# Two matmul stages on one core: a part of the weight preparation is moved behind the sums of an item

## The chip, the cores and the metric

The kernel runs on one core of a Trainium2 chip. The core has five engines that run side by side, each with its own queue of instructions in program order: PE (TensorE, the matmul engine, with a separate record PEld for its weight loads), DVE (VectorE), ACT (ScalarE), POOL (GpSimd) and SP (SyncE, which starts the transfers here). An engine waits where an operand that another engine makes is not there yet, and everything behind the waiting instruction on that engine waits too. The metric is the device time of one execution in microseconds. Three timed runs of the kernel before took 768.05, 769.60 and 771.38 us: 769.6 is the median.

## The reference

Attention with a learned bias over positions, and behind it a two-layer network with a squared relu, all in float32. `_attn_ref` makes `attn_out` of 4 batches x 8 heads x 576 positions x 64; it is laid out as `x` of 2304 tokens x 512, and then:

```python
def _moe_ref(x, w_in, w_out):
    h = x @ w_in              # 512 -> 2048
    r = np.maximum(h, 0.0)
    g = r * r
    return (g @ w_out)        # 2048 -> 512
```

In the attention part `scores = scale * q k^T + bias`, where the bias is a small network of the distance of two positions, then softmax and a product with `v`. The change leaves that part alone.

## The kernel before

The first half of the program (to some 376 us) is the attention part; beside it eight of the sixteen `w_in` tiles are prepared. The second half is a loop over 40 items, written by hand in the order in which each engine is to run it (`with tc.manual_schedule()`, L954 on): no scheduler reorders it.

An item is a pair (n, P): n is a block of tokens (four of 512, worked as 256 columns by a seven-product scheme, and a fifth, half as wide, of what is left), P is one of eight pieces of the hidden dimension. `runs` says in which order they come: items 0 to 3 are block 0 with P 0 to 3, items 4 to 7 block 1, 8 to 11 block 2, 12 to 17 block 3, and so on; the last eight items are the narrow block. For an item i the loop issues

- `products(i)`: on PE, 24 matmuls into the PSUM tile `ha` and 18 into `hb` (L851). Both tiles exist once, so they can be written only when the sums of item i-1 have read them.
- `parts_g(i - 1)`: the squared result of the item before is split in a high part `gh` (a cast on ACT, L887) and the rest `gl` (a subtraction on DVE, L888), two halves each.
- `lead(m)` for the weight tiles m that `lead_at` gives this item: one ACT operation (L176) and four DVE operations on the bits of a raw weight tile (L179 to L182) that put together the tile `wa`.
- `sums(i)`: ACT writes `s` from `ha` (L865), and four DVE operations (L867 to L870) combine `ha`, `hb` and `s` to `c`. The first two read `ha`, the others `hb`.
- `high_out(m)` for a `w_out` tile: a cast on ACT (L778) and a subtraction on POOL (L779). For a `w_in` tile: `sums_in` on POOL (L789 to L791), `high_in` on ACT (L800), `low_in` on DVE (L804), and the fetch of the next raw tile.
- `high_x`, `low_x`, `sums_x` in the items of `split_at`: the split of a coming block of tokens (L825 on ACT, L832 on DVE, L819 on POOL).
- `squares(i)`: relu and square on ACT (L876, L877) for items below `GA`, one DVE operation (L879) for the others.
- `down(i - 1)`: on PE, 24 matmuls into `y` for a full-width item (L943), with `gh`, `gl` and the two `w_out` tiles of the piece. Behind the last item of a run, `leave` copies `y` out.

A block's scale is found in two steps. `x_largest` (four DVE reductions, L185) stands in items 4, 8 and 28; `set_scale` stands in the item after. The latter calls `power` (L187): one more small reduction on DVE (L185), a one-column matmul that spreads the result over the partitions (L194, into a free column of `hb`), and four tiny DVE operations that read it (L195 to L199) and one more (L600). The matmul L194 stands on PE between `products(i)` and `down(i - 1)`.

In the kernel before, `set_scale` is issued ahead of `parts_g`, and all the `lead` calls of an item ahead of its `sums`. Items 1, 2 and 3 have two `w_out` tiles each; items 4, 5, 8, 9, 12 to 15 and 18 to 25 have one tile each.

Of the kernel before, what the change touches and what calls it, by code (L numbers as in the profile page):

```python
# [36 lines left out]
MD, K0, E2, BW, KP, PN, KA = 0x15555, 2, 1, 1, 2, 1, 1  # L37
C0, ND, NG, GA, QA, WU, QS = 2, 2, 4, 18, 12, 32, 2
BO, B1 = (3, 5, 8, 10, 13, 15, 18, 20), (12, 3, 8)
# [12 lines left out]
AH = 2  # L52
ND = 3
NG = 4
GA = 26
KA = 4
QA = 0
WU = 12
# [19 lines left out]
def attention_then_relu2_mlp(ctx: ExitStack, tc: tile.TileContext, q, k, v, cols, w_in, w_out, psi, xmat, dist, out):  # L78
# [92 lines left out]
    def lead_w(n, a):  # L171

        raw = wraw_t.pop(n)
        low, high = (raw[:, :, :, t] for t in range(2))
        af = a.bitcast(F32)
        ins = ACT.activation(out=af, in_=high.bitcast(F32), func=AF.Abs)  # L176
        if n in early:
            tc.keep_in_program_order(ins)
        DVE.tensor_scalar(out=af, in0=af, scalar1=HI_MIN, scalar2=HI_MAX, op0=ALU.max, op1=ALU.min)  # L179
        DVE.tensor_scalar(out=a, in0=a, scalar1=3, scalar2=0x3FFFFFFF, op0=ALU.logical_shift_left, op1=ALU.bitwise_and)  # L180
        DVE.scalar_tensor_tensor(out=a, in0=high, scalar=-0x40000000, in1=a, op0=ALU.bitwise_and, op1=ALU.bitwise_or)  # L181
        DVE.scalar_tensor_tensor(out=a.bitcast(U32), in0=low.bitcast(U32), scalar=29, in1=a.bitcast(U32), op0=ALU.logical_shift_right, op1=ALU.bitwise_or)  # L182
# [55 lines left out]
    def is_in(n):  # L238
        return n // 2 % 2 == 0
# [344 lines left out]
    def take(x, o, n):  # L584
        o += 18 * S * x
        return area[:, o:o + n]
# [65 lines left out]
    for s in range(NU + TL + 1):  # L652
# [43 lines left out]
        if s < AB * HP * TAIL:  # L696
            n, r = divmod(s, AB * HP)
# [33 lines left out]
    NI = len(items)  # L731
# [3 lines left out]
    stays = (4, 7)  # L735

    lead_at = {1: (6, 7), 2: (10, 11), 3: (14, 15)}
    lead_at.update(zip((4, 5, 8, 9, 12, 13, 14, 15), ((n,) for n in range(16, 24))))
    lead_at.update(zip(range(18, 26), ((n,) for n in range(24, 32))))
    split_at = {0: (1, (2, 5, 3, 4)), 3: (1, (1, 6, 7))}  # L740
    split_at.update({i + j: (n, ms) for i, n in ((6, 2), (10, 3), (30, B)) for j, ms in enumerate(((2, 5, 3, 4), (1, 6, 7)))})
# [14 lines left out]
    def fetch_out(n):  # L756
        fetch(n, home[n].tile([128, 1024], F32, name=f"r{n}", tag=f"w{n}", bufs=1))
# [11 lines left out]
    def lead(n):  # L769
        a = stage_p["p"].tile([128, 2, 256], F32, name="wa", tag="wa", bufs=2)  # L770
        lead_w(n, a.bitcast(I32))
        scratch[n] = a

    def high_out(n):
        a = scratch[n].rearrange("p g n -> p (g n)")
        t = home[n].tile([128, 2, 512], F32R, name=f"w{n}", tag=f"w{n}", bufs=1)
        hi, lo = t[:, 0], t[:, 1]
        ACT.copy(hi, a)  # L778
        POOL.tensor_tensor(out=lo, in0=a, in1=hi.bitcast(F32), op=ALU.subtract)  # L779
        w_t[n] = (hi, lo)  # L780

    def blocks_in(n):
        a = scratch[n].rearrange("p g (a b) -> p (g a) b", b=128)
        return a, zraw[n][:, 0:640].rearrange("p (a b) -> p a b", b=128)

    def sums_in(n):
        a, z = blocks_in(n)
        tt = POOL.tensor_tensor
        tt(out=z[:, 0:2], in0=a[:, 0:2], in1=a[:, 2:4], op=ALU.subtract)  # L789
        tt(out=z[:, 2:4], in0=a[:, 1:3], in1=a[:, 2:4], op=ALU.add)  # L790
        tt(out=z[:, 4], in0=a[:, 0], in1=a[:, 3], op=ALU.add)  # L791
# [47 lines left out]
    def products(i):  # L839
        n, P = items[i]  # L840
        w = width[n]
        ha = ph_p.tile([128, 4, 256], F32, name="ha", tag="ha")
        hb = ph_p.tile([128, 4, 256], F32, name="hb", tag="hb")
        for ms, h in (((2, 3, 4, 5), ha), ((1, 6, 7), hb)):
            for s, m in enumerate(ms):
                k = 0
                for c in range(2):
                    wh, wl = (x[:, LEFT[m]] for x in w_t[4 * P + c])
                    xh, xl = (x[:, c] for x in xs_t[n, m])
                    for a, x in ((wh, xh), (wh, xl), (wl, xh)):  # L850
                        PE.matmul(h[:, s, :w], lhsT=a, rhs=x, start=(k == 0), stop=(k == 5))  # L851
                        k += 1
        return ha, hb

    def sums(i, ha, hb):
        n, P = items[i]
        w = width[n]
        alpha = alpha_t[n]
        if i % 2:
            c, s = (take(1, o, 1024).rearrange("p (m t) -> p m t", m=4)[:, :, :w] for o in (4480, 5504))  # L860
        elif i < NP // 2:
            c, s = (tmp_p.tile([128, 4, 256], F32, name=x, tag=x) for x in "cs")
        else:
            c, s = (xT[1][:, :, 256 * x:256 * x + w] for x in range(2))
        ACT.activation(out=s, in_=ha[:, :, :w], func=AF.Identity, scale=alpha)  # L865
        stt = DVE.scalar_tensor_tensor
        stt(out=c[:, 2:4], in0=ha[:, 1:3, :w], scalar=alpha, in1=s[:, 0:4:3], op0=ALU.mult, op1=ALU.subtract)  # L867
        stt(out=c[:, 0:2], in0=ha[:, 2:4, :w], scalar=alpha, in1=s[:, 0:2], op0=ALU.mult, op1=ALU.add)
        stt(out=c[:, 2:4], in0=hb[:, 0:1, :w].to_broadcast([128, 2, w]), scalar=alpha, in1=c[:, 2:4], op0=ALU.mult, op1=ALU.add)
        stt(out=c[:, 2:4], in0=hb[:, 1:3, :w], scalar=alpha, in1=c[:, 2:4], op0=ALU.mult, op1=ALU.add)  # L870
        c_t[i] = c

    def squares(i):
        c = c_t[i]
        if i < GA:
            ACT.activation(out=c, in_=c, func=AF.Relu)  # L876
            ACT.activation(out=c, in_=c, func=AF.Square)  # L877
        else:
            DVE.scalar_tensor_tensor(out=c, in0=c, scalar=0.0, in1=c, op0=ALU.max, op1=ALU.mult)  # L879

    def parts_g(i):
        c, w = c_t[i], width[items[i][0]]
        for f in range(2):
            gh = mlp.tile([128, 2, 256], F32R, name="gh", tag="gh", bufs=2)[:, :, :w]
            gl = mlp.tile([128, 2, 256], F32R, name="gl", tag="gl", bufs=2)[:, :, :w]
            g = c[:, 1 - f:4:2]
            ACT.copy(gh, g)  # L887
            DVE.tensor_tensor(out=gl, in0=g, in1=gh.bitcast(F32), op=ALU.subtract)  # L888
            g_t[i, f] = (gh, gl)
# [64 lines left out]
    with tc.manual_schedule():  # L954
        for n in first_outs:
            fetch_out(n)
        for n in (6, 7, 10, 11, 14, 15):
            fetch_out(n)
        fetch_in(raw_ins.pop(0))
        sums_x(*split_at[0])  # L960
        for n in first_outs:
            lead(n)
            high_out(n)
        for i in range(NI + 1):
            if i == NP // 2:
                tmp_stack.close()
                late = ctx.enter_context(tc.tile_pool(name="late", bufs=1, side="right", reuse_waits="tile"))
                home.update({n: late for n in (4 * NP - 2, 4 * NP - 1)})
            n, P = items[min(i, NI - 1)]
            if i:  # L970
                fetch_y(i - 1)
            if i < NI:
                ha, hb = products(i)
            if scales and scales[0][0] == i:
                _, m, cols = scales.pop(0)
                set_scale(m, cols, hb[:, 3, 0:1])
            if i:
                parts_g(i - 1)
            for m in lead_at.get(i, ()):
                lead(m)  # L980
            if i < NI:
                sums(i, ha, hb)
            for m in lead_at.get(i, ()):
                if is_in(m):
                    sums_in(m)
                else:
                    high_out(m)
            if i in split_at:
                high_x(*split_at[i])
            if i == 12:  # L990
                keep_tails()
            for m in lead_at.get(i, ()):
                if is_in(m):
                    high_in(m)
                    low_in(m)
                    if raw_ins:
                        fetch_in(raw_ins.pop(0))
            if 4 <= i and raw_outs:
                fetch_out(raw_outs.pop(0))
            if i in split_at:  # L1000
                low_x(*split_at[i])
            if i + 1 in split_at:
                sums_x(*split_at[i + 1])
            if i in largest_at:
                scales.append((i + 1, largest_at[i], x_largest(largest_at[i])))
            if i < NI:
                squares(i)
            if i < NI and (n, P) in firsts:
                r = run_of[n, P]
                if P == 0 and n < B:  # L1010
                    store_x(n)
                if r + 2 < len(runs) and runs[r + 1][1] and r + 1 not in stays:
                    load_x(runs[r + 1][0])
            if i:
                down(i - 1)
# [50 lines left out]
```

## Time and profile before

| | |
|---|---|
| timed runs | 768.05, 769.60, 771.38 us |
| profiled execution, its own time | 769.3 us |
| its span, first to last instruction | 767.5 us |
| mean granted TensorE clock | 0.97 |
| PE busy | 718.7 us, 94% |
| DVE busy | 556.6 us, 73% |
| ACT busy | 463.1 us, 60% |
| POOL busy | 171.8 us, 22% |

The span leaves 1.8 us of the execution outside. The busy share is a mean over the two halves of the program, which have different limits, so what counts for a part of the program is where PE stands idle in it and what ended that. [...] Matmul ends are modelled, so the start of one matmul to the start of the next says more than a single duration.

### The profile page before, as it was taken

Reading aid. Unit: us, or ns where it says so; the run is one execution under the profiler, and the core shown is the slowest. Engines: PE = TensorE matmul, PEld = TensorE weight load, DVE = VectorE, ACT = ScalarE, POOL = GpSimd, SP = SyncE. Lnnn points to the kernel's source line nnn. Section 1 sums busy time; section 2 is a strip of 40 time slices with the busy share of each in tenths; the row PEclk is TensorE's granted clock in tenths of the full one; section 3 lists DMA queues with packets and bytes.
Section 4 is the critical chain, followed back from the end, with each engine's and each line's share of the span. In section 5 each row is a group of like instructions: output and inputs, shape, how many; then the busy total and the mean of one; then the engine's idle time right before and its main releaser. Section 6 shows DMA issues by size and latency. Waiting matters only on the chain.

```text
span 767.5 us, 18176 instructions
## 1 busy us (share of the span) xinstructions
PE 718.7 (94%) x7382; PEld 576.5 (75%) x7382; DVE 556.6 (73%) x1184; ACT 463.1 (60%) x934; POOL 171.8 (22%) x281
## 2 busy tenths in 40 slices
PE   6889999999989999879988999999999999999992
PEld 5767877877756777657776787888888888878881
DVE  6689878775767677897588896777458876669651
ACT  4367787877646678878665685776466554223220
POOL 1464333231210023452014230401001111001000
PEclk7599999999999999999999999999999999999997
DMA  7530000000487522200530446032018332533100
GB/s 212 171 91 18 5 15 2 3 2 18 118 301 225 188 63 88 86 28 2 169 120 1 172 172 233 1 122 86 1 55 312 112 126 97 206 110 111 56 2 27
DMA packets 31607, 75.33 MB, mean 98 GB/s; under 512 B 5540, under 2 KB 13732, under 8 KB 30500
## 3 DMA queue, kind: packets, MB, share of 16 engines
q1 hardware_dynamic: 31524, 74.17, 28.4%
q8 instruction: 58, 0.95, 0.5%
q14 instruction: 25, 0.20, 0.1%
HBM read 55.81 MB, written 18.35 MB: 97 GB/s over the span
## 4 chain that ended last, share of the span: by engine, by line
PE 74%; DVE 12%; ACT 4%; DMA 3%; issue 3%; POOL 2%; SPq 0%; DVEq 0%; ACTq 0%; POOLq 0%
PE y L943 24%; PE ha L851 11%; PE px L505 9%; PE sp L431 8%; PE hb L851 8%; PE pp L487 6%; PE bb L379 4%; DMA stage<-in_w_in 2%; PE bb L398 2%; DVE mask L368 1%; DVE t L437 1%; DVE wa L181 1%; ACT p L442 1%; PE pa L490 1%; ACT pt L488 1%
## 5 line engine op out<-in xcount | busy, mean ns | idle before, releaser
L943 PE MATMUL y<-w,gh 128*128 128x512 f32 x576 | 182.1, 397 | 0.3 <-ACT gh L887 0.2
L851 PEld LDWEIGHTS <-area 128*128 128x128 f16 x1680 | 148.5, 98 | 31.8 <-issue 8.7
L442 ACT ACTIVATE p<-t,negm 128x576 f32<-128x576 f32 x144 | 111.1, 774 | 25.1 <-DVE negm L437 25.0
L437 DVE CUSTOM_DVE_ANT_0 t<-sp,area 128x576 f32<-128x576 f32 x144 | 103.9, 751 | 29.8 <-PE sp L431 25.4
L943 PEld LDWEIGHTS y<-w,gh 128*128 128x128 f32 x576 | 105.2, 188 | 21.4 <-ACT gh L887 0.8
L943 PE MATMUL y<-w,gl 128*128 128x512 f32 x288 | 113.4, 394 | 2.3 <-DVE gl L888 2.3
L431 PE MATMUL sp<-k,q 64*128 64x288 f32 (+1 forms) x640 | 103.2, 432 | 10.2 <-DVE negm L437 6.3
L488 ACT COPY pt<-pp 128x512 f32<-128x512 f32 x144 | 79.5, 582 | 35.3 <-PE pp L487 35.0
L505 PE MATMUL px<-pt,v 128*64 128x128 f32 (+1 forms) x1600 | 97.3, 267 | 2.6 <-DVE bt L385 1.2
L505 PEld LDWEIGHTS px<-pt,v 128*64 128x64 f32 x1600 | 79.5, 137 | 19.5 <-issue 6.4
L851 PE MATMUL ha<-area 128*128 128x256 f16 (+1 forms) x816 | 86.4, 263 | 5.7 <-ACT area L825 2.2
L487 PE MATMUL pp<-ident,p 128*128 128x128 f32 x576 | 84.3, 283 | 2.8 <-ACT pt L488 1.2
L431 PEld LDWEIGHTS sp<-k,q 64*128 64x128 f32 (+1 forms) x640 | 54.5, 177 | 32.1 <-issue 10.6
L487 PEld LDWEIGHTS pp<-ident,p 128*128 128x128 f32 x576 | 62.1, 142 | 20.4 <-issue 10.5
L390 POOL TENSOR_TENSOR area<-bt,bt 128x256 f32<-128x256 f32 x72 | 54.2, 776 | 73.2 <-DVE bt L385 73.2
L368 DVE TENSOR_TENSOR mask<-sdist,theta 128x1024 f16<-128x1024 f16 x81 | 55.8, 725 | 14.8 <-PE bb L398 8.7
L943 PEld LDWEIGHTS y<-w,gl 128*128 128x128 f32 x288 | 54.1, 188 | 16.3 <-DVE gl L888 4.5
L851 PE MATMUL hb<-area 128*128 128x256 f16 (+1 forms) x612 | 64.7, 260 | 0.0
L888 DVE TENSOR_TENSOR gl<-area,gh 128x512 fp32r<-128x512 f32 (+1 forms) x40 | 25.1, 655 | 32.6 <-ACT gh L887 30.9
L779 POOL TENSOR_TENSOR w<-wa,w 128x512 fp32r<-128x512 f32 x16 | 20.9, 1307 | 115.0 <-ACT w L778 115.0
L379 PE MATMUL bb<-wmov,mask 128*128 128x64 f16 x1152 | 40.7, 196 | 0.5 <-DVE bt L385 0.3
L379 PEld LDWEIGHTS <-mask 128*128 128x128 f16 x1152 | 37.0, 100 | 5.4 <-issue 3.9
(171 smaller groups left out, 970.6 us busy)
## 6 DMA issues: line engine op xcount, KB each, us to landing
stage<-in_w_in SPq DMA_DIRECT2D x24, 512.0 KB, 4.3
r<-in_w_out SPq DMA_DIRECT2D x16, 512.0 KB, 5.6
xs<-area SPq DMA_DIRECT2D x4, 1792.0 KB, 9.7
py<-o SPq DMA_DIRECT2D x12, 512.0 KB, 3.5
o<-py SPq DMA_DIRECT2D x12, 512.0 KB, 4.1
v<-in_v SPq DMA_DIRECT2D x16, 320.0 KB, 4.0
q<-in_q SPq DMA_DIRECT2D x32, 128.0 KB, 3.5
zw<-in_w_in SPq DMA_DIRECT2D x8, 512.0 KB, 3.5
```

The source lines that it names most:

```text
L368: DVE.tensor_tensor(out=out, in0=win, in1=th, op=ALU.is_ge)
L379: PE.matmul(bb[:, 64 * (7 - r):64 * (8 - r)], lhsT=m[:, r], rhs=wmov[:, n], start=(n == 0), stop=(n == 1))
L390: POOL.tensor_tensor(out=dst, in0=tw, in1=sw, op=ALU.add)
L431: mm = PE.matmul(out_t[to, x, :HALF], lhsT=qt[rows, cols], rhs=kt[rows, k0:k0 + HALF], start=True, stop=True)
L437: DVE.tensor_tensor_reduce(out=t.rearrange("p (x n) -> p x n", x=2), in0=sp[:, :, :HALF], in1=bias.rearrange("p (x n) -> p x n", x=2), sca ...
L442: ACT.activation(out=p[:, S * n:S * n + S], in_=t, func=AF.Exp, bias=negm[:, n:n + 1], scale=-1.0, accum_out=sums[:, 2 * ic + n:2 * ic + n ...
L487: PE.transpose(pp[:, 128 * c:128 * c + 128], p[:, k0:k0 + 128], ident)
L488: ACT.copy(pt[:, 4 * h:4 * h + 4], pp.rearrange("p (c m) -> p c m", c=4))
L505: PE.matmul(px[64 * h:64 * h + 64, :w], lhsT=vt[:, c, h], rhs=src, start=(c == 0), stop=(c == 4))
L851: PE.matmul(h[:, s, :w], lhsT=a, rhs=x, start=(k == 0), stop=(k == 5))
L888: DVE.tensor_tensor(out=gl, in0=g, in1=gh.bitcast(F32), op=ALU.subtract)
L943: PE.matmul(y_t[n][k], lhsT=a[:, slot, o:o + 128], rhs=x, start=((n, P) in firsts and f == 0 and m == 0), stop=((n, P) in lasts and f == 1 ...
```

## The change

There are four edits. In an item with two weight tiles the first one's bit operations stay ahead of `sums`, and the second's go behind it; the second's cast and subtraction go behind `squares`. `set_scale` is issued behind `sums` instead of ahead of `parts_g`. The table `lead_at` gives no tile to items 4 and 8, and two tiles to items 14 and 15. `GA` is 32 instead of 26, so items 26 to 31 have relu and square on ACT.

```diff
--- before.py
+++ after.py
@@ -52,7 +52,7 @@
 AH = 2
 ND = 3
 NG = 4
-GA = 26
+GA = 32
 KA = 4
 QA = 0
 WU = 12
@@ -735,7 +735,7 @@
     stays = (4, 7)
 
     lead_at = {1: (6, 7), 2: (10, 11), 3: (14, 15)}
-    lead_at.update(zip((4, 5, 8, 9, 12, 13, 14, 15), ((n,) for n in range(16, 24))))
+    lead_at.update({5: (16,), 9: (17,), 12: (20,), 13: (21,), 14: (18, 19), 15: (22, 23)})
     lead_at.update(zip(range(18, 26), ((n,) for n in range(24, 32))))
     split_at = {0: (1, (2, 5, 3, 4)), 3: (1, (1, 6, 7))}
     split_at.update({i + j: (n, ms) for i, n in ((6, 2), (10, 3), (30, B)) for j, ms in enumerate(((2, 5, 3, 4), (1, 6, 7)))})
@@ -971,20 +971,20 @@
                 fetch_y(i - 1)
             if i < NI:
                 ha, hb = products(i)
+            if i:
+                parts_g(i - 1)
+            one, *two = lead_at.get(i, (None,))
+            if one is not None:
+                lead(one)
+            if i < NI:
+                sums(i, ha, hb)
             if scales and scales[0][0] == i:
                 _, m, cols = scales.pop(0)
                 set_scale(m, cols, hb[:, 3, 0:1])
-            if i:
-                parts_g(i - 1)
-            for m in lead_at.get(i, ()):
+            if one is not None:
+                (sums_in if is_in(one) else high_out)(one)
+            for m in two:
                 lead(m)
-            if i < NI:
-                sums(i, ha, hb)
-            for m in lead_at.get(i, ()):
-                if is_in(m):
-                    sums_in(m)
-                else:
-                    high_out(m)
             if i in split_at:
                 high_x(*split_at[i])
             if i == 12:
@@ -1005,6 +1005,8 @@
                 scales.append((i + 1, largest_at[i], x_largest(largest_at[i])))
             if i < NI:
                 squares(i)
+            for m in two:
+                high_out(m)
             if i < NI and (n, P) in firsts:
                 r = run_of[n, P]
                 if P == 0 and n < B:
```

On DVE, in item 2 (`c` and `s` are its sums, `r_6547` and `r_6549` the raw tiles of its two `w_out` tiles), the program stands so before:

```order
L179 TENSOR_SCALAR wa<-wa 128x512
L180 TENSOR_SCALAR wa<-wa 128x512
L181 SCALAR_TENSOR_TENSOR wa<-r_6547,wa 128x512
L182 SCALAR_TENSOR_TENSOR wa<-r_6547,wa 128x512
L179 TENSOR_SCALAR wa<-wa 128x512
L180 TENSOR_SCALAR wa<-wa 128x512
L181 SCALAR_TENSOR_TENSOR wa<-r_6549,wa 128x512
L182 SCALAR_TENSOR_TENSOR wa<-r_6549,wa 128x512
L867 SCALAR_TENSOR_TENSOR c<-ha,small,s 128x512
L868 SCALAR_TENSOR_TENSOR c<-ha,small,s 128x512
L869 SCALAR_TENSOR_TENSOR c<-hb,small,c 128x512
L870 SCALAR_TENSOR_TENSOR c<-hb,small,c 128x512
```

and so now:

```order
L179 TENSOR_SCALAR wa<-wa 128x512
L180 TENSOR_SCALAR wa<-wa 128x512
L181 SCALAR_TENSOR_TENSOR wa<-r_6547,wa 128x512
L182 SCALAR_TENSOR_TENSOR wa<-r_6547,wa 128x512
L867 SCALAR_TENSOR_TENSOR c<-ha,small,s 128x512
L868 SCALAR_TENSOR_TENSOR c<-ha,small,s 128x512
L869 SCALAR_TENSOR_TENSOR c<-hb,small,c 128x512
L870 SCALAR_TENSOR_TENSOR c<-hb,small,c 128x512
L179 TENSOR_SCALAR wa<-wa 128x512
L180 TENSOR_SCALAR wa<-wa 128x512
L181 SCALAR_TENSOR_TENSOR wa<-r_6549,wa 128x512
L182 SCALAR_TENSOR_TENSOR wa<-r_6549,wa 128x512
```

The four sums moved ahead of the second tile's four bit operations; items 1 and 3 read alike.

On DVE around the scale in item 5 (`xT_4285` is the block whose largest value is sought, `xT_77` the result of item 4, `zw` the raw `w_in` tile), before:

```order
L804 SCALAR_TENSOR_TENSOR area<-zw,small,area 128x640
L185 TENSOR_REDUCE small<-xT_4285 128x1 x4
L185 TENSOR_REDUCE small<-small 128x1
L195 TENSOR_SCALAR small<-hb 128x1
L197 TENSOR_SCALAR small<-small 128x1
L198 TENSOR_SCALAR small<-small 128x1
L199 TENSOR_SCALAR small<-small 128x1
L600 TENSOR_TENSOR small<-small 128x1
L888 TENSOR_TENSOR gl<-xT_77,gh 128x512 x2
L179 TENSOR_SCALAR wa<-wa 128x512
L180 TENSOR_SCALAR wa<-wa 128x512
L181 SCALAR_TENSOR_TENSOR wa<-zw,wa 128x512
```

and now:

```order
L185 TENSOR_REDUCE small<-xT_4285 128x1 x4
L888 TENSOR_TENSOR gl<-xT_77,gh 128x512 x2
L179 TENSOR_SCALAR wa<-wa 128x512
L180 TENSOR_SCALAR wa<-wa 128x512
L181 SCALAR_TENSOR_TENSOR wa<-zw,wa 128x512
L182 SCALAR_TENSOR_TENSOR wa<-zw,wa 128x512
L867 SCALAR_TENSOR_TENSOR area<-ha,small,area 128x512
L868 SCALAR_TENSOR_TENSOR area<-ha,small,area 128x512
L869 SCALAR_TENSOR_TENSOR area<-hb,small,area 128x512
L870 SCALAR_TENSOR_TENSOR area<-hb,small,area 128x512
L185 TENSOR_REDUCE small<-small 128x1
L195 TENSOR_SCALAR small<-hb 128x1
```

The small reduction `small<-small` and what follows it moved behind `gl`, the bit operations and the four sums of item 5. In item 9 it is the same; in item 29 there are no bit operations. 

On PE at the same place in item 5 (with what each instruction waits for), before:

```order
L851 MATMUL hb<-area 128x256
L194 MATMUL hb<-small,ones 128x1 [waits DVE_49]
L943 MATMUL y_7163<-w_6565,gh 128x512 [waits Activation_49]
L943 MATMUL y_7163<-w_6565,gh 128x512
L943 MATMUL y_7163<-w_6565,gl 128x512 [waits DVE_49]
```

and now:

```order
L851 MATMUL hb<-area 128x256
L194 MATMUL hb<-small,ones 128x1 [waits DVE_49]
L943 MATMUL y_7148<-w_6565,gh 128x512 [waits Activation_49]
L943 MATMUL y_7148<-w_6565,gh 128x512
L943 MATMUL y_7148<-w_6565,gl 128x512
```

The order on PE did not move: L194 still waits for DVE ahead of the first `y`. What DVE has to do before it is another thing now, and `gl` needs no wait of its own any more.

On ACT the second `abs` (L176) of items 1 to 3 moved behind the first cast, and the second cast (L778) from ahead of relu and square (L876, L877) to behind them, ahead of `gh` (L887).

## Rows read from the trace of the kernel before

**Rows 1.** Windows: from:to, length, busy PE PEld DVE ACT POOL, PEclk, DMA, GB/s
```profile
381.70:419.40 37.70, 32.66 (x199) 26.03 (x200) 30.98 (x47) 21.65 (x31) 10.74 (x9) 0.95 0.21 76
441.10:451.20 10.10, 10.10 (x68) 8.46 (x68) 9.83 (x13) 9.12 (x12) 4.12 (x4) 1.00 0.79 302
429.50:441.10 11.60, 10.85 (x70) 8.68 (x69) 10.60 (x23) 7.96 (x13) 2.23 (x4) 1.00 0.72 275
471.40:483.00 11.60, 10.69 (x70) 8.59 (x70) 6.50 (x15) 4.16 (x7) 1.70 (x2) 1.00 0.63 226
674.70:686.20 11.50, 10.59 (x69) 8.61 (x68) 7.50 (x16) 2.17 (x3) 0.00 (x0) 1.00 0.52 182
```

**Rows 2.** PE timeline: start, length, engine, line, operands, count, [idle before, releaser]
```profile
218.42 1.24 PE L431 MATMUL sp<-k,q 64*128 64x288 f32 x8 [2.48 <-DVE negm L437]
...
340.95 1.24 PE L431 MATMUL sp<-k,q 64*128 64x288 f32 x8 [2.30 <-DVE negm L437]
...
394.31 4.42 PE L851 MATMUL ha<-area 128*128 128x256 f16 x24 [2.10 <-DVE area L868]
...
419.35 2.79 PE L851 MATMUL ha<-area 128*128 128x256 f16 x24 [2.25 <-ACT area L825]
...
471.35 2.79 PE L851 MATMUL ha<-area 128*128 128x256 f16 x24
...
475.95 0.28 PE L194 MATMUL hb<-small,ones 128*128 128x1 f32 x2
...
477.71 0.50 PE L943 MATMUL y<-w,gl 128*128 128x512 f32 x1 [0.91 <-DVE gl L888]
```

**Rows 3.** DVE timeline of item 1
```profile
386.04 1.29 DVE L888 TENSOR_TENSOR gl<-c,gh 128x512 fp32r<-128x512 f32 x2 [0.27 <-issue]
...
390.42 1.79 DVE L181 SCALAR_TENSOR_TENSOR wa<-r,wa 128x512 int32<-128x512 int32 x1
...
392.85 0.74 DVE L867 SCALAR_TENSOR_TENSOR area<-ha,small,area 128x512 f32<-128x512 f32 x1
...
394.94 0.75 DVE L870 SCALAR_TENSOR_TENSOR area<-hb,small,area 128x512 f32<-128x512 f32 x1
```

**Rows 4.** DVE timeline of items 8, 9 and 29
```profile
470.50 0.16 DVE L185 TENSOR_REDUCE small<-small 128x1 f32<-128x4 f32 x1
...
478.18 0.42 DVE L179 TENSOR_SCALAR wa<-wa 128x512 f32<-128x512 f32 x1
...
480.43 0.74 DVE L867 SCALAR_TENSOR_TENSOR area<-ha,small,area 128x512 f32<-128x512 f32 x1
...
684.43 1.23 DVE L879 SCALAR_TENSOR_TENSOR area<-area 128x1024 f32<-128x1024 f32 x1
```

**Rows 5.** POOL timeline of item 1
```profile
390.37 1.29 POOL L779 TENSOR_TENSOR w<-wa,w 128x512 fp32r<-128x512 f32 x1 [17.62 <-ACT w L778]
```

**Rows 6.** ACT timeline behind the sums of item 1
```profile
395.73 1.06 ACT L876 ACTIVATE area<-area 128x1024 f32<-128x1024 f32 x1 [2.10 <-DVE area L870]
...
397.90 1.14 ACT L887 CAST gh<-area 128x512 fp32r<-128x512 f32 x2
```

**Rows 7.** ACT timeline of item 9
```profile
472.08 1.17 ACT L887 CAST gh<-xT 128x512 fp32r<-128x512 f32 x2
473.12 0.70 ACT L176 ACTIVATE wa<-r 128x512 f32<-128x512 f32 x1
474.18 1.11 ACT L865 ACTIVATE area<-ha,small 128x1024 f32<-128x1024 f32 x1 [0.36 <-PE ha L851]
```

**Rows 8.** Windows behind the four PE gaps over 2 us after start-up
```profile
220.20:223.20 3.00, 3.00 (x15) 2.01 (x15) 2.38 (x7) 1.99 (x5) 0.00 (x0) 0.50 1.03 414
341.00:344.00 3.00, 3.00 (x37) 2.31 (x37) 2.79 (x8) 2.68 (x8) 2.51 (x4) 1.00 0.45 160
394.30:397.30 3.00, 2.99 (x15) 2.07 (x16) 1.36 (x2) 1.54 (x2) 0.67 (x1) 0.50 0.00 0
419.40:422.40 3.00, 3.00 (x28) 2.68 (x29) 2.96 (x5) 2.72 (x4) 0.63 (x1) 1.00 0.00 0
```

## The prediction

> **What bounds the kernel now.** I read the page's busy rows first: TensorE (PE) 94% busy over the span, VectorE (DVE) 73%, ScalarE (ACT) 60%. The diff touches only the second half of the program, the loop over 40 items, so I cut that half by item. An item that nothing disturbs takes 10.1 us and PE is busy in all of it; items 1 to 3 together take 37.7 us with PE idle for 5 us; items 5, 9 and 29 take 11.6, 11.6 and 11.5 us [rows 1]. No other full-width item has a gap, so these six are the places where time can be won or lost, and a change elsewhere has to lengthen something past 10.1 us before it is seen.
>
> Then the PE timeline says what those gaps are [rows 2]. Items 2 and 4 begin late because `ha` may not be overwritten before the sums of the item before have read it; the second of these is put down to an ACT operation that ends when the sums do. In items 5, 9 and 29 the scale of a coming block is computed: a one-column matmul (L194) stands behind `hb`, and the down product behind it waits 0.9 us for `gl` (item 9; about as long in 5 and 29).
>
> **The first edit: the second tile's bit operations go behind the sums (items 1 to 3).** On DVE item 1 now runs gl, four bit operations, four more, then sums [rows 3]. The first sum starts at 392.85, and what PE waits for is the second (L868). The second set of bit operations is dear because its L181 takes 1.79 us, against 0.7 for the same line in a set that runs alone (start to start of the set 478.18 to 480.43 is 2.25 us, [rows 4]); GpSimd (POOL) subtracts the first tile's low half from 390.37 to 391.66 [rows 5], and DVE's operation ends only after it. Putting the sums ahead of that set takes about 3.4 us from the way to `ha`, more than the longest gap of 2.25 us, so these gaps go. If nothing else became late the three items would take 3 x 10.1 = 30.3 us, a gain of 7.4.
>
> What is late next is the ring through the second tile: end of sums, relu and square 2.17 us (395.73 to 397.90), a cast for the second tile of about 0.6 (it now stands between square and `gh`), `gh` 0.6 for its first half [rows 6], gl 1.29, one set of bit operations 2.25, sums 2.84 (392.85 to 394.94 and 0.75) [rows 3, 4]: 9.8 us, below 10.1. But POOL subtracts the second tile right when gl wants to start, for 1.29 us [rows 5], while gh lasts 0.6: gl can be held some 0.6 us more, and the ring is 10.4. Adding the one 1.1 us hold that L181 shows gives 11.5. I take 0.6 us of remaining wait in each of three items, 1.8 in all (0 to 4.2). So the first edit gives -5.6 us (-7.4 to -3.2). The 1.6 us of slow clock in item 2 (below) is already in the 37.7.
>
> [...]
>
> **The same edit moves the scale behind the sums (items 5, 9 and 29), and this is the costly part.** Before, the small reduction that L194 reads came directly behind the reductions of the block, an item early: at 470.50, with PE asking at 475.95 [rows 2, 4]. It now stands on DVE behind gl, one set of bit operations and four sums of the item itself. L194 still stands on PE ahead of the down product, so all 24 of its matmuls queue behind a wait on DVE.
> Item 9, with ha at 471.35: gh ends at 473.25 and abs at 473.82 [rows 7]; gl can be through by 473.9; bit operations 2.25 us to 476.15; sums 2.84 to 479.0; reduction 0.17 and 0.05 of signalling (as from 395.69, the end of L870, to ACT's 395.73) to 479.2. PE stood ready at 475.95: a wait of 3.3 us. With 0.14 for L194 itself (half of the 0.28 of its two passes) the period is 10.1 + 0.14 + 3.3 = 13.5 against 11.6: **+1.9**.
> Item 5 is the same with DVE and ACT still behind: the ring of items 1 to 3 runs at its limit, and in item 3 low_x (three operations of 0.7 us) and three scaled copies stand in it too. Item 4 has no set of bit operations, which gives 2.25 back. I estimate 0 to 2.3 us of lateness and take 1.6: wait 4.9, period 15.1 against 11.6: **+3.5** (+1.9 to +4.2).
> Item 29 has no bit operations. Its sums cannot start before s, which in item 9 ends 3.9 us behind the start of ha (475.29, [rows 7]); + 2.84 + 0.2 = 7.0, and L194 could have run at 4.6: a wait of 2.4. Period 12.6 against 11.5: **+1.1**.
> The old 0.9 us wait for gl goes in all three, as these periods include.
>
> **The clock.** [...] In the first half a gap of 2.48 us was followed by 0.50, one of 2.30 by 1.00 [rows 2, 8]. So two of the four gaps over 2 us behind the start-up cost 1.63 us each, and no gap of 3 to 5 us occurs in that stretch. The new waits are 4.9, 3.3 and 2.4 us long, and DVE is not the limit behind them, so the loss would not be hidden as it was in item 2. I count one drop for each, 3 x 1.63 = **+4.9** (0, if the gaps fall as two of the four did, to 7, if the longest costs two).
>
> **Edits that I cost at nothing.** Items 4 and 8 lose a set of bit operations: inside 10.1 us that PE fills, so no gain beside the one counted in item 5. Items 14 and 15 get two sets: the same ring of 9.8 to 10.4 us, at most 0.6 together, hidden by the slack that the items before build. The tiles 16 to 23 are used from item 16 on, so none comes late. Six squares of 1.23 us leave DVE [rows 4] for two ACT operations of 2.17 us in items 26 to 31; ACT has nothing else urgent there and the result is wanted about a product later, behind 4.6 us of PE work, which covers the 0.9 us more. If that cover were gone, 6 x 0.9 = 5 us. The queue of transfers only shifts places; the fetch of tile 17 is needed four items later than before, so no transfer becomes late.
>
> **Sum.** -5.6 + 1.9 + 3.5 + 1.1 + 4.9 = +5.8 us. The profiled execution took 769.3 us (span 767.5 and 1.8 around it), within 0.3 of the median 769.6: 775.1 us.
>
> **Rivals.**
> *The waits come, the clock stays up.* For it: gaps of 2.25 and 2.30 us left it at 1.00. Against: the new ones are longer. -5.6 + 6.5 = +0.9: 770.2 us.
> *The waits are longer.* If item 5 is 2.3 us late (+0.7), the ring holds items 1 to 3 at 1.4 us each (+2.4), and the longest gap costs two drops (+1.6), 4.7 more: 779.8 us. [...]
> *L194 does not hold the down product: faster.* It is one instruction with one column; if PE took up y behind it, or the reduction came early, the three old waits of 1.5 us would go as well: -5.6 - 4.5 = -10.1, 759.2 us. It decides the sign once the mean wait per scale is below 3.2 us without clock losses (3 x (3.2 + 0.14 - 1.5) = 5.6), or below 1.6 us with one each. Against it: in [rows 2] PE takes y only after L194, and the order above keeps the reduction behind the sums. [...]
> *The edit moves the gap only:* the second tile's cast, now behind square, lets the down product wait for its low half, and items 1 to 3 keep 2 us each. Its low half is ready about S + 4.1 us (2.2, 0.6, 1.3) where S is the end of the sums, and the second half of y starts later than that. With the rest as forecast 779 us; I put it with the second rival.
>
> **How the numbers follow.** A measurement of this kernel can tell 0.5% (3.85 us) from no change. Forecast 0.62, its own range 772 to 778.5; clock stays up 0.18; longer waits 0.12; L194 holds nothing 0.08. Slower by over 0.5% (above 773.4): three quarters of the forecast (0.47) and the longer waits (0.12), 0.59. Within 0.5%: the other quarter (0.15) and the steady clock (0.18), 0.33. Faster: 0.08. The range from 769.5 to 779.5 leaves out the fast rival and the upper end of the long one.
>
> **What would show it.** In the changed profile: ha of items 2 to 4 without a gap over 1 us; before the down product of items 4, 8 and 28 (periods 5, 9 and 29) a PE wait that ends with the DVE reduction L185 by way of L194, about 4.9, 3.3 and 2.4 us; behind each a stretch of granted clock 0.5; periods of about 10.7, 15, 13.5 and 12.6 us before clock losses; items 14, 15 and 26 to 31 without gaps, 29 aside. I am wrong if L194 starts right behind hb, if items 1 to 3 stay at 12.6 us, or if gaps turn up in items 14 to 18 or 26 to 31.

## The result, and the profile after

Six runs of the changed kernel took 774.3 to 782.5 us, median 778.2, against 769.75 for the kernel before: slower by 1.06% (ratio 1.0106, 95% interval 1.0067 to 1.0146). 775.1 us was forecast, with a range to 779.5. The profiled execution took 777.1 us with a span of 775.0, 7.5 us more than before.

On the page PE is busy 2.5 us longer than before with the same number of instructions (721.2 us against 718.7 before), so the larger part of the 7.5 us is idle time:

```profile
PE 721.2 (93%) x7382; PEld 578.6 (75%) x7382; DVE 553.9 (71%) x1178; ACT 476.5 (61%) x946; POOL 170.7 (22%) x281
```

By item, the windows that answer to [rows 1] (from:to, length, busy time of PE, PEld, DVE, ACT and POOL, granted clock as a share of full speed, DMA share, GB/s) are these of the changed kernel; items 1, 2, 3, 4, 5, 6, 9 and 29 in turn (item 0 begins at 378.05):

```profile
383.50:393.80 10.30, 10.30 (x66) 8.37 (x66) 9.86 (x16) 6.97 (x10) 1.30 (x1) 1.00 0.89 329
393.80:404.10 10.30, 10.30 (x67) 8.38 (x67) 8.86 (x15) 6.55 (x9) 2.82 (x3) 1.00 0.00 2
404.10:416.90 12.80, 10.60 (x67) 8.38 (x66) 11.36 (x15) 7.56 (x11) 6.39 (x5) 1.00 0.01 1
416.90:428.70 11.80, 10.45 (x68) 8.45 (x67) 11.66 (x18) 7.43 (x11) 1.73 (x1) 1.00 0.37 156
428.70:445.20 16.50, 12.26 (x70) 9.92 (x70) 10.35 (x20) 8.73 (x15) 5.53 (x6) 0.90 0.30 117
445.20:455.30 10.10, 10.10 (x68) 8.48 (x68) 6.56 (x10) 6.94 (x10) 1.21 (x1) 1.00 0.45 176
475.40:489.20 13.80, 10.72 (x69) 8.70 (x68) 10.21 (x19) 7.70 (x11) 5.58 (x6) 1.00 0.26 91
681.00:693.70 12.70, 10.51 (x69) 8.63 (x68) 6.31 (x15) 4.42 (x6) 0.00 (x0) 1.00 0.48 165
```

Items 1 and 2 are down to 10.3 us, under the 10.7 that was forecast for each of items 1 to 3; item 3 has stayed at 12.8, and item 4 has grown from 10.1 to 11.8. Items 5, 9 and 29, at 11.6, 11.6 and 11.5 before, have grown to 16.5, 13.8 and 12.8. What ended PE's gaps in that half is one wait, three times, and a few smaller ones (us in total, times, the longest; the small wait of item 1 for L868 was there before):

```profile
PE hb L194 <- DVE small L185: 9.5, 3, 4.2
PE y L943 <- ACT gh L887: 1.6, 1, 1.6
PE hb L851 <- DVE area L832: 1.4, 2, 0.9
PE ha L851 <- DVE c L868: 0.7, 1, 0.7
PE y L943 <- DVE gl L888: 0.7, 1, 0.7
```

The chain that ended last shows what stands in front of the longest of them, in item 5 (start, us, what). Each step takes its turn on DVE: gl, four bit operations, four sums, and only then the small reduction; PE had ended `hb` at 433.45.

```profile
431.87 0.68 DVE gl L888
...
434.12 0.69 DVE wa L182
434.81 0.66 DVE area L867
...
436.05 0.75 DVE area L869
...
436.82 0.75 DVE area L870
437.57 0.08 DVE small L185
...
437.69 0.56 PE hb L194 x2
438.25 6.86 PE y L943 x23
```

The same rows for items 9 and 29 on PE, which answer to L194 in [rows 2]:

```profile
483.29 0.38 PE L194 MATMUL hb<-small,ones 128*128 128x1 f32 x2 [3.08 <-DVE small L185]
```

```profile
687.91 0.38 PE L194 MATMUL hb<-small,ones 128*128 128x1 f32 x2 [2.19 <-DVE small L185]
```

The old waits for gl behind L194 are gone, as forecast.

### The profile page after: what moved, and what is told of

Its sections match the earlier page's. It is cut to its first block, busy times and chain, and to the rows that moved or that the text cites. A ratio compares the mean times of both kernels' runs of the same rounds, so it can differ in the third digit from the quotient of the medians.

```text
span 775.0 us, 18186 instructions
## 1 busy us (share of the span) xinstructions
PE 721.2 (93%) x7382; PEld 578.6 (75%) x7382; DVE 553.9 (71%) x1178; ACT 476.5 (61%) x946; POOL 170.7 (22%) x281
## 4 chain that ended last, share of the span: by engine, by line
PE 72%; DVE 15%; ACT 4%; issue 4%; DMA 3%; POOL 1%; SPq 0%; ACTq 0%; DVEq 0%
PE y L943 23%; PE ha L851 10%; PE px L505 9%; PE sp L431 9%; PE hb L851 7%; PE pp L487 7%; PE bb L379 4%; DMA stage<-in_w_in 2%; PE bb L398 2%; DVE t L437 2%; DVE mask L368 1%; PE pa L490 1%; DVE wa L181 1%; ACT p L442 1%; ACT pt L488 1%
## 5 line engine op out<-in xcount | busy, mean ns | idle before, releaser
L943 PE MATMUL y<-w,gh 128*128 128x512 f32 x576 | 183.2, 399 | 1.6 <-ACT gh L887 1.6
L851 PEld LDWEIGHTS <-area 128*128 128x128 f16 x1680 | 147.7, 98 | 27.2 <-issue 11.4
L943 PEld LDWEIGHTS y<-w,gh 128*128 128x128 f32 x576 | 106.0, 190 | 23.2 <-ACT gh L887 2.3
L431 PE MATMUL sp<-k,q 64*128 64x288 f32 (+1 forms) x640 | 105.3, 440 | 9.9 <-DVE negm L437 5.8
L943 PE MATMUL y<-w,gl 128*128 128x512 f32 x288 | 113.6, 394 | 0.7 <-DVE gl L888 0.7
L851 PE MATMUL ha<-area 128*128 128x256 f16 (+1 forms) x816 | 84.8, 260 | 0.7 <-DVE c L868 0.7
L851 PE MATMUL hb<-area 128*128 128x256 f16 (+1 forms) x612 | 65.0, 260 | 1.4 <-DVE area L832 1.4
L943 PEld LDWEIGHTS y<-w,gl 128*128 128x128 f32 x288 | 54.3, 189 | 13.9 <-DVE gl L888 1.9
L888 DVE TENSOR_TENSOR gl<-area,gh 128x512 fp32r<-128x512 f32 (+1 forms) x40 | 25.9, 668 | 36.4 <-ACT gh L887 34.7
```

Source lines behind the costliest of these rows:

```text
L431: mm = PE.matmul(out_t[to, x, :HALF], lhsT=qt[rows, cols], rhs=kt[rows, k0:k0 + HALF], start=True, stop=True)
L943: PE.matmul(y_t[n][k], lhsT=a[:, slot, o:o + 128], rhs=x, start=((n, P) in firsts and f == 0 and m == 0), stop=((n, P) in lasts and f == 1 ...
```

## The experiments

Each kernel has four to twelve timed runs, beside runs of the kernel before on the same chip. The first four experiments, the next three and the last two ran on a chip each (the kernel before had medians of 770.0, 770.3 and 771.0 us there), so kernels of different chips are compared by their ratios. The table gives the median, the ratio to the kernel before with its 95% interval, and, from the one profile of each, the time from one start of `ha` to the next: items 1 to 4 together, then 5, 9 and 29. The row "before" is that of the chip of the changed kernel.

| kernel | us | ratio | 1 to 4 | 5 | 9 | 29 |
|---|---|---|---|---|---|---|
| before | 769.8 | 1 | 47.7 | 11.6 | 11.6 | 11.5 |
| changed | 778.2 | 1.0106 (1.0067 to 1.0146) | 45.2 | 16.5 | 13.8 | 12.8 |
| scale back | 766.5 | 0.9958 (0.9943 to 0.9974) | 45.2 | 11.6 | 11.6 | 11.5 |
| scale alone | 786.0 | 1.0210 (1.0189 to 1.0232) | 47.8 | 19.0 | 13.8 | 12.8 |
| reduction early | 777.7 | 1.0108 (1.0089 to 1.0128) | 45.2 | 16.4 | 15.2 | 12.7 |
| sets alone | 767.6 | 0.9961 (0.9947 to 0.9976) | 45.2 | 11.6 | 11.6 | 11.5 |
| scale half way | 764.9 | 0.9935 (0.9914 to 0.9956) | 45.2 | 12.2 | 11.0 | 10.3 |
| matmul early | 763.1 | 0.9909 (0.9889 to 0.9929) | 45.2 | 10.4 | 10.4 | 10.3 |
| cast behind gh | 763.1 | 0.9904 (0.9883 to 0.9924) | 43.2 | 10.4 | 10.4 | 10.3 |
| POOL sums early | 763.4 | 0.9903 (0.9886 to 0.9921) | 44.6 | 10.4 | 10.4 | 10.3 |
| both | 762.0 | 0.9884 (0.9865 to 0.9903) | 43.3 | 10.4 | 10.4 | 10.3 |

**Scale back.** The changed kernel with `set_scale` where it was.

```diff
                 ha, hb = products(i)
+            if scales and scales[0][0] == i:
+                _, m, cols = scales.pop(0)
+                set_scale(m, cols, hb[:, 3, 0:1])
             if i:
                 parts_g(i - 1)
...
                 sums(i, ha, hb)
-            if scales and scales[0][0] == i:
-                _, m, cols = scales.pop(0)
-                set_scale(m, cols, hb[:, 3, 0:1])
```

> The changed kernel with the scale put back ahead of parts_g; all else stays changed. Theory (the one-column matmul L194 waits for DVE and the down product queues behind it): the three L194 waits of 4.2, 3.1 and 2.2 us go and the old gl waits of 0.5 to 0.9 us come back, items 5, 9 and 29 take about 11.6 us each instead of 16.5, 13.8 and 12.8, items 1 to 4 stay at about 45.2 us together: some 766 to 768 us, below the kernel before (769.7). Rival (the moved bit operations, the table or the squares cost the time, the scale is innocent): stays near 778.

766.5 us, as the theory had it; the three items are back at 11.6, 11.6 and 11.5. The whole loss sits in this one edit, and what is left of the change gains 0.4%.

**Scale alone.** The kernel before with `set_scale` moved behind `sums` and nothing else.

```diff
-            if scales and scales[0][0] == i:
-                _, m, cols = scales.pop(0)
-                set_scale(m, cols, hb[:, 3, 0:1])
             if i:
                 parts_g(i - 1)
...
                 sums(i, ha, hb)
+            if scales and scales[0][0] == i:
+                _, m, cols = scales.pop(0)
+                set_scale(m, cols, hb[:, 3, 0:1])
```

> The kernel before with one edit alone: the scale behind the sums. Theory: L194 waits of 3 to 4 us in items 5 and 9 and 2 to 3 us in item 29, +2 to +3, +2 and +1.3 us, and 0 to 5 us more where the granted clock falls to 0.5 behind them: 775 to 780 us. Rival (the scale is innocent): 769.7.

786.0 us: the right way, and more than expected. Item 5 is the reason. With the old table item 4 still has a weight tile of its own, whose four bit operations stand on DVE ahead of the sums of item 4 (425.80 to 428.13), so DVE comes still later to item 5: its gl starts 5.1 us behind the first `ha` of item 5, against 2.6 in the changed kernel. The wait is 6.8 us instead of the 3 to 4 expected:

```profile
441.99 0.58 PE L194 MATMUL hb<-small,ones 128*128 128x1 f32 x2 [6.77 <-DVE small L185]
```

Behind so long a wait the granted clock was at 0.5 while PE still stood, and stayed there after (windows of the same kernel, columns as above):

```profile
438.60:441.60 3.00, 0.00 (x0) 0.00 (x0) 2.96 (x5) 0.91 (x2) 2.26 (x4) 0.51 0.95 398
442.00:445.00 3.00, 3.00 (x8) 2.52 (x9) 2.28 (x6) 2.03 (x3) 2.87 (x3) 0.50 0.49 198
```

The profiled run was the fastest of the five (781.2 us); what the others lost beyond it no trace shows, but their mean granted clocks were lower, 0.956 to 0.961 against 0.965.

By these rows the empty item 4 is worth some 2.5 us of wait in item 5 (6.77 against 4.24) beside the moved scale. That is read from the rows and not tested alone: the order in items 1 to 3 differs between these two kernels too. The empty item 8 is worth nothing: item 9 takes 13.8 us with and without it. Beside the old place of the scale the whole table is worth nothing that these runs can tell: "scale back" (0.9943 to 0.9974), with the new table and the six squares on ACT, and "sets alone" (0.9947 to 0.9976), without them, have the same periods.

**Reduction early.** The changed kernel with the small reduction back at the end of the item before.

```diff
             if i in largest_at:
-                scales.append((i + 1, largest_at[i], x_largest(largest_at[i])))
+                top = column()
+                largest(x_largest(largest_at[i]), top)
+                scales.append((i + 1, largest_at[i], top))
```

> The changed kernel with one DVE operation moved: the small reduction that L194 reads goes back to the end of the item before, the four operations that read L194's result stay behind the sums. Theory (it is the place of this one reduction on DVE): no L194 wait and no gl wait either, items 5, 9 and 29 at 10.2 to 10.5 us, items 1 to 4 about 45.2: 762 to 765 us. Rival (the whole chain of scale operations behind the sums delays DVE, or L194 waits for the sums' reading of hb): L194 still waits 3 us, 775 or more.

777.7 us: the theory fell here, the rival was right. L194 waits as long as before, but now for L870, the last of the four sums, which starts at 435.33 and reads `hb`:

```profile
436.13 0.38 PE L194 MATMUL hb<-small,ones 128*128 128x1 f32 x2 [4.17 <-DVE area L870]
```

```profile
435.33 0.75 DVE L870 SCALAR_TENSOR_TENSOR area<-hb,small,area 128x512 f32<-128x512 f32 x1
```

L194 writes into `hb`, and it is issued behind the sums that read `hb`, so it waited for them too (three waits, 9.3 us in all), though it writes a column that they don't read. There were two locks on the same door; the reduction's place was only the one that the profile named, since it came last. (That the place of the matmul behind the sums is the second lock, "matmul early" below tests; whether the wait is laid on the whole tile or on a part of it, no run tells.)

**Sets alone.** The kernel before with the second tile's bit operations behind the sums and its cast behind the squares; the diff is that of the change without the lines on `GA`, `lead_at` and `set_scale`.

> The kernel before with one edit alone: in items 1 to 3 the second tile's bit operations behind the sums and its cast behind the squares. Theory: gaps ahead of ha in items 2 to 4 (2.1, 0.7, 2.2 us) go, 1 to 3 us of them come back as waits in items 3 and 4, item 5 starts some 2.5 to 4 us earlier: 766 to 768 us. Rival (the edit only moves the gap, from ha to the down product): 769 to 771.

767.6 us, as expected: 2.5 us of the gaps of items 1 to 4 are gone (47.7 to 45.2).

**Scale half way.** The changed kernel with `set_scale` behind the bit operations and ahead of the sums.

```diff
                 lead(one)
+            if scales and scales[0][0] == i:
+                _, m, cols = scales.pop(0)
+                set_scale(m, cols, hb[:, 3, 0:1])
             if i < NI:
                 sums(i, ha, hb)
-            if scales and scales[0][0] == i:
-                _, m, cols = scales.pop(0)
-                set_scale(m, cols, hb[:, 3, 0:1])
```

> The changed kernel with the scale half the way back: behind gl and the bit operations, ahead of the sums. Theory (PE waits for whatever stands ahead of the scale on DVE, operation by operation): the wait ahead of the down product shrinks by the 2.8 us of the sums, from 4.2 to 1.4 us in item 5, from 3.1 to 0.2 in item 9, from 2.2 to none in item 29: 766 to 769 us. Rival (the scale costs by being behind parts_g at all): 774 or more.

The waits fell to 1.46 and 0.32 us and in item 29 to none, by 2.8, 2.8 and 2.2 us. That is the length of the four sums where there was so much to take away. 764.9 us is 1 us under the expectation.

```profile
430.74 0.38 PE L194 MATMUL hb<-small,ones 128*128 128x1 f32 x2 [1.46 <-DVE small L185]
```

```profile
472.03 0.38 PE L194 MATMUL hb<-small,ones 128*128 128x1 f32 x2 [0.32 <-DVE small L185]
```

**Matmul early.** "Reduction early", with the one-column matmul issued right behind the products; the five operations behind it stay where the change put them. (`spread` tells `power` that the matmul has been issued.)

```diff
                 ha, hb = products(i)
+            if scales and scales[0][0] == i:
+                PE.matmul(hb[:, 3, 0:1], lhsT=ones, rhs=scales[0][2], start=True, stop=True)
...
-        PE.matmul(ps_col, lhsT=ones, rhs=cols, start=True, stop=True)
+        if not spread:
+            PE.matmul(ps_col, lhsT=ones, rhs=cols, start=True, stop=True)
```

> The changed kernel with the small reduction at the end of the item before and the one-column matmul issued ahead of the sums, right behind the products; only the four operations that read its result stay behind the sums. Theory (two locks, the reduction's place on DVE and the sums' reading of the tile hb into which the matmul writes; the experiment before took away the first alone and the matmul then waited 3 to 4 us for L870): no wait of the matmul, none for gl; items 5, 9 and 29 at 10.2 to 10.5 us, 761 to 764 us. Rival (the read of its result behind the sums holds something else): 766 or more.

763.1 us, as expected. With both locks off, the matmul (now L976) stands with no wait, and gl needs none behind it, because nothing of the scale stands in front of it any more; what is left are the wait ahead of item 1 and those of item 3. (The lines of this kernel are one further down: L944 is the L943 of before, L852 its L851.)

```profile
432.97 0.28 PE L976 MATMUL hb<-small,ones 128*128 128x1 f32 x2
```

```profile
PE y L944 <- ACT gh L888: 1.6, 1, 1.6
PE ha L852 <- DVE c L869: 0.7, 1, 0.7
PE y L944 <- DVE gl L889: 0.7, 1, 0.7
```

The wait of item 4's `hb` for low_x is missing in this list, yet items 1 to 4 take 45.2 us as before. In this execution item 3 took 14.4 us, and item 4 then found low_x done and took 10.2: 24.6 us for the two, as in the changed kernel (12.8 and 11.8). "Reduction early" shows the same, with 14.2 and 10.4, and there the granted clock was at 0.50 in item 3 (window of that kernel):

```profile
409.90:412.90 3.00, 2.59 (x6) 2.12 (x7) 2.90 (x6) 1.06 (x2) 0.00 (x0) 0.50 0.00 0
```

The slow stretch of PE cost nothing there (24.6 us for the two items in all three kernels): PE would have waited for DVE right behind it.

So the idea of the change, operations of the scale behind the sums, is good for some 3 us against "scale back" (ratios 0.9909 and 0.9958, whose intervals do not meet; 3.6 us in the periods of items 5, 9 and 29), if the part that PE waits for is left ahead.

**What is left in items 3 and 4.** In the changed kernel the second tile's bit operations of item 2 take 4.7 us (404.45 to 409.19) instead of 2.25, beside three POOL sums that item 3 needs (L819); the cast waits for them, and gh queues behind the cast. DVE, POOL and ACT of the changed kernel, in this order:

```profile
404.45 0.92 DVE L179 TENSOR_SCALAR wa<-wa 128x512 f32<-128x512 f32 x1
405.41 1.38 DVE L180 TENSOR_SCALAR wa<-wa 128x512 int32<-128x512 int32 x1
406.82 1.63 DVE L181 SCALAR_TENSOR_TENSOR wa<-r,wa 128x512 int32<-128x512 int32 x1
408.49 0.70 DVE L182 SCALAR_TENSOR_TENSOR wa<-r,wa 128x512 uint32<-128x512 uint32 x1
```

```profile
403.81 1.27 POOL L819 TENSOR_TENSOR area<-xT 128x512 f32<-128x512 f32 x1
405.05 2.86 POOL L819 TENSOR_TENSOR xT<-xT 128x512 f32<-128x512 f32 x2
```

```profile
409.22 0.62 ACT L778 CAST w<-wa 128x512 fp32r<-128x512 f32 x1 [2.50 <-DVE wa L182]
409.75 1.14 ACT L887 CAST gh<-c 128x512 fp32r<-128x512 f32 x2
```

Two edits were tried on top of "matmul early", alone and together. **Cast behind gh**: the cast and subtraction of the second tile are issued behind `parts_g` of the next iteration.

```diff
             if i:
                 parts_g(i - 1)
+                for m in after_gh:
+                    high_out(m)
...
-            for m in two:
-                high_out(m)
+            after_gh = two
```

> The kernel of the run before this one with the cast and subtraction of the second weight tile behind gh of the same item instead of ahead of it (items 1 to 3). Theory (in item 2 the bit operations beside three POOL sums take 4.7 us instead of 2.25, the cast waits for them and gh queues behind the cast, so PE waits 1.6 and 0.7 us): gh comes 2 us earlier, gl then still waits for DVE's bit operations; the period of item 3 falls by about 1 us, 760 to 763 us. Rival (gl on DVE is the limit, or the subtraction now comes late for the second half of the down product): no change, or up to 2 us more.

**POOL sums early**: the three sums at the end of item 0.

```diff
+            if i == 0:
+                sums_x(*split_at[3])
-            if i + 1 in split_at:
+            if i + 1 in split_at and i != 2:
                 sums_x(*split_at[i + 1])
```

> The kernel with the early one-column matmul (761 to 765 us), and the three POOL sums that item 3 needs issued at the end of item 0 instead of item 2. Theory (these three sums hold the second tile's bit operations of item 2, which take 4.7 us instead of 2.25, and that is what makes gh late in item 3): the bit operations of item 2 are back at 2.25 us, the waits of 1.6 and 0.7 us in item 3 go or shrink under 0.5; the sums now meet gl or bit operations of item 1, which have about 1 us of slack: the items 1 to 4 shorter by 1 to 2 us in all. Rival (the cast and the ring itself are the limit, POOL is not): item 3 stays at 12.8 us or the gap turns up in item 1 in full.

**Both** of them.

> Both edits on top of the early matmul: the second tile's cast behind gh, and the three POOL sums at the end of item 0. Theory: items 1 to 4 at 10.1 to 10.8 us each but for the wait of hb in item 4 for low_x, 759 to 762 us. Rival (each edit moves the same gap and they do not add): as the better of the two, 761 to 763.

By the profiles the first takes 2.0 us from items 1 to 4, the second 0.6, both 1.9: they do not add, as the rival of "both" had it (its time, 762.0, lies in both ranges). By the measured times none can be told from "matmul early" (ratios 0.9904, 0.9903 and 0.9884 against 0.9909, with intervals of 0.4%), so for the first the rival "no change" is not excluded; its profiled run was the fastest of its five. The second shows the mechanism cleanly: the bit operations of item 2 are back at 2.2 us (405.16 to 407.4), and the hold has moved to gl of item 0, 3.12 us instead of 1.29, beside the same sums (DVE, then POOL; L889 and L820 are the L888 and L819 of before):

```profile
386.68 3.12 DVE L889 TENSOR_TENSOR gl<-c,gh 128x512 fp32r<-128x512 f32 x2 [0.27 <-issue]
...
405.16 0.42 DVE L179 TENSOR_SCALAR wa<-wa 128x512 f32<-128x512 f32 x1
405.61 0.43 DVE L180 TENSOR_SCALAR wa<-wa 128x512 int32<-128x512 int32 x1
406.07 0.69 DVE L181 SCALAR_TENSOR_TENSOR wa<-r,wa 128x512 int32<-128x512 int32 x1
406.80 0.69 DVE L182 SCALAR_TENSOR_TENSOR wa<-r,wa 128x512 uint32<-128x512 uint32 x1
```

```profile
385.83 3.42 POOL L820 TENSOR_TENSOR xT<-xT 128x512 f32<-128x512 f32 x2 [12.44 <-DVE area L833]
```

The expected 1 to 2 us did not come (0.6). Against the changed kernel, item 3 is 2.4 us shorter (10.4 instead of 12.8), but items 1 and 2 are 1.8 longer (11.05 and 11.4 instead of 10.3 each). In item 4 a wait of `hb` for low_x, some 1.4 us, stays in both edits. "Both" has the lowest median, 762.0 us, 1.2% under the kernel before; the changed kernel is 1.1% over it.

## Why the prediction was right, step by step

*What bounds it, and the sign.* Right but for item 4: the six items named moved, and item 4, which was not named, grew by 1.6 us; all other full-width items kept their length (item 6 above is one). From the start of item 0 to the end, the periods account for 5.8 us of the 7.5 in the profile (-2.5 + 4.9 + 2.2 + 1.3). The other 1.8 us were lost ahead of item 0, which began at 378.05 instead of 376.29. PE, DVE and ACT have the same order up to there in all eleven kernels, and item 0 begins anywhere from 373.9 us ("scale half way") to 378.05, so these 1.8 us are spread between executions and not the change. One part of it shows: behind a gap of 2.27 us that ended at 342.26 the clock was at 0.50, where it had stayed at 1.00 behind the 2.30 us at the same place before (second lines of [rows 2] and [rows 8]; window of the changed kernel):

```profile
342.30:345.30 3.00, 3.00 (x24) 2.03 (x26) 1.82 (x4) 2.70 (x8) 2.50 (x4) 0.50 0.43 156
```

That 5.8 is also the sum I had forecast is luck: the first edit gave 3.1 us less than its term, and the clock cost 3.3 us less than its term, and the two cancel. By the medians the change cost 8.4 us.

*The first edit, forecast -5.6 us: measured -2.5.* In items 1 to 3, where I counted it, it gave -4.2 (37.62 to 33.45), inside its range; item 4, which I did not count here, gave 1.6 back. Items 1 and 2 did what was said, and gl beside POOL's subtraction (397.10, 1.27 us) took 1.95 us for its pair instead of 1.29, near the 0.6 I had added as an estimate (POOL's 1.29 us less the 0.6 of gh):

```profile
397.57 1.95 DVE L888 TENSOR_TENSOR gl<-area,gh 128x512 fp32r<-128x512 f32 x2 [1.20 <-ACT gh L887]
```

What I had not put in the ring were the three POOL sums of item 2, which meet the moved bit operations, +2.4 us, so that item 3 stayed at 12.8, and the wait of item 4's `hb` for low_x, 0.49 and 0.86 us. My 1.8 us beyond 10.1 in three items was 4.8 us in four (45.2 against 40.4).

*The scale in items 5, 9 and 29, forecast waits 4.9, 3.3 and 2.4 us: measured 4.24, 3.08 and 2.19.* All three waits were a little shorter; by periods, +3.5, +1.9 and +1.1 were forecast and +4.9 (with 1.6 us of slow clock in it), +2.2 and +1.3 came. I had also misread the old wait for gl in item 5: it was 0.51 us and not about 0.9 like the others. The cause as I gave it, the reduction's place on DVE, was half of it: "reduction early" took it away and kept the wait, and only with the matmul ahead of the sums did it go. The forecast of the time did not depend on it, a repair would have.

*The clock, forecast one drop behind each wait, +4.9.* The 1.63 us of a drop were read from one gap (4.42 us of ha at 0.50 against 2.79 at 1.00, third and fourth lines of [rows 2] and [rows 8]); three of them were an estimate. In the profiled execution only the longest wait was followed by 0.50; behind the other two it stayed at 1.00 (windows right behind the three waits):

```profile
437.80:440.80 3.00, 3.00 (x8) 2.44 (x9) 2.40 (x7) 1.92 (x2) 2.67 (x3) 0.50 0.00 0
483.40:486.40 3.00, 3.00 (x14) 2.48 (x15) 2.58 (x7) 1.93 (x2) 2.72 (x3) 1.00 0.00 0
688.00:691.00 3.00, 3.00 (x15) 2.51 (x16) 0.69 (x5) 1.94 (x2) 0.00 (x0) 1.00 0.04 18
```

So 1.6 us of it show there (without its wait, item 5 took 12.26 us and item 9 took 10.71). The six runs had mean granted clocks from 0.957 (782.5 us, the slowest) to 0.969 (774.3 and 775.2 us, the two fastest), so the clock may well have a part in their spread of 8 us; but the runs without a profile don't say where it fell, and whether the forecast's 4.9 us come in other executions stays open.

*Edits costed at nothing.* Right: items 8, 14, 15 and 26 to 31 (29 aside) have 10.05 to 10.1 us as before, and "scale back" against "sets alone" finds nothing in the table and in `GA`.

*The rivals.* "L194 does not hold the down product" is refuted by the profile (PE stood 4.24, 3.08 and 2.19 us ahead of L194 and took no matmul of y in that time), and by "scale half way" operation for operation. "The clock stays up" was true of two waits in the one profile. "The waits are longer" lies nearer to the measured 778.2 (779.8) than the forecast does, but only its ring came true, 4.8 us beyond 10.1 where it said 4.2; the waits for the scale were shorter and not longer, and no two falls of the clock followed the longest. "The gap moves only" was right in item 3, though by another way: there PE waited 1.55 us for gh, which queued behind the late cast, and not for the tile's low half. Of the 7.4 us a third, 2.5, were kept.

## What to carry to other kernels

Here a one-column matmul on the busiest engine was a gate for everything queued behind it: the 24 matmuls of y behind L194 began only after its waits of 4.24, 3.08 and 2.19 us. Moving the little chain that it belongs to to a slack place on another engine also moved the time at which the gate opened (786.0 us for that edit alone, against 770.0 on the same chip). Split such a chain at the matmul, leave what feeds it early and move only what reads it (763.1 us); and look for every operand and every tile that it touches, since the profile named just the wait that ended last, and behind the lifted one the next was as long (4.17 us for L870 after 4.24 for L185). Where an order written by hand puts operations on two engines that hold each other up, as DVE's bit operations beside POOL's sums did here (4.7 us instead of 2.25), count all their meetings in the new order, not the one that the old trace happens to show.

## What the hardware showed beyond that

Beside POOL's sums DVE's operations with one tile to read (`wa<-wa`) were held as well, not only L181 with its two (`wa<-r,wa`; 1.63 us instead of 0.69): L179 and L180 of item 2 took 0.92 and 1.38 us instead of 0.42 and 0.43 (rows above). A tiny operation was held too: L601 of "POOL sums early", an operation on two one-column operands, took 1.23 us, to 437.64, beside the second of two POOL sums that ended at 437.61, where L600 took 0.16 alone in item 5 before. The tiny operations with one operand just ahead of it, beside the same POOL sums, were not held (0.14 to 0.15 us each):

```profile
436.23 0.14 DVE L200 TENSOR_SCALAR small<-small 128x1 f32<-128x1 f32 x1
436.41 1.23 DVE L601 TENSOR_TENSOR small<-small 128x1 f32<-128x1 f32 x1
```

```profile
435.06 2.55 POOL L820 TENSOR_TENSOR xT<-xT 128x512 f32<-128x512 f32 x2
```

And the length of a gap alone did not decide the clock. The wait of item 9, about the same in three kernels (3.08, 3.09 and 3.02 us), was followed by 1.00 in the changed kernel and in "scale alone", and by 0.50 in "reduction early":

```profile
481.70:484.70 3.00, 3.00 (x8) 2.52 (x9) 2.32 (x6) 2.05 (x2) 2.81 (x3) 0.50 0.00 0
```

All three waits over 4 us (4.17, 4.24 and 6.77) were followed by 0.50; of the gaps of 2.1 to 2.3 us some were (2.10 in the kernel before, 2.27 in the changed kernel) and some were not (2.19 in the changed kernel, 2.25 and 2.30 in the kernel before).
